# Three-stage kernel: attention's small matmuls with PE's halves in turn, and leaky relu kept in the PSUM bank of h

## The chip, the cores and the metric

The kernel runs on one core of a Trainium2 chip. Its time is the device time of one execution in microseconds (us); the kernel before was run three times for the median, and one further execution was profiled.

## The reference

Input are q, k, v of 4 batches x 8 heads x 576 positions x 64, and the weights of two MLP layers ("MoE 1" and "MoE 2") of width 512 -> 2048 -> 512, in float64. What is computed, cut to what matters:

```python
scores = (q @ k.T) / 8                          # per batch and head
rel = pos[:, None] - pos[None, :]
plain   = (rel >= 0) & (rel < 32)               # heads 0 to 3
dilated = (rel >= 0) & (rel < 128) & (rel % 4 == 0)   # heads 4 to 7
x = softmax(where(mask, scores, -1e9)) @ v      # -> 2304 tokens x 512

h = x @ w_in1                                   # MoE 1: 2304 x 2048
g = maximum(h, 0) + alpha * minimum(h, 0)       # leaky relu, one slope per column
x = g @ w_out1

h = x @ w_in2                                   # MoE 2
g = (a0 + a1 h + a2 h^2 + a3 h^3) / (1 + |b0||h| + |b1|h^2 + 1e-6)
out = g @ w_out2
```

## The kernel before

The matmuls of the MLP layers run in a fast fp32 format, each operand split in a high and a low part, so that every product is three matmuls (low x high, high x low, high x high). Attention's matmuls run in plain fp32; each of them appears in the trace as two.

**Chunks and jobs.** The 2304 tokens are cut in 8 chunks of 288 (u = 0 to 7). One attention job (`attention_job`, a generator with a `yield` between its stages) does one pair of heads of one chunk: `hp` 0 and 1 are plain, 2 and 3 dilated. Its stages are: load q and k; turn them with PE (L354 to L364); copy them to SBUF on ScalarE (ACT); load v; scores; row maxima on VectorE (DVE, `maxima`, L421); exponentials on ACT; row sums inverted on DVE and applied on GpSimd (POOL, `norm`); turn the weights with PE (`turn`); copy (`turned`); P V (L500 to L514); split the result in the high and low part of x1 (L523, L524).

**Scores.** A dilated job has 4 blocks per head; each head has its own PSUM bank, and `scores(0)` and `scores(1)` are separate stages. A head lies on 64 of the 128 partitions, so its matmuls use half of PE's rows (64 x 72 weights, with 72 columns for even u and 104 for odd u). A plain job has 5 blocks; both heads are done by one matmul each, with the queries of the two heads in `qz`, a 128 x 128 block with zeros off its diagonal halves: `scores(0)` does all, `scores(1)` nothing.

**P V.** Both heads write to one bank, head 0 to partitions 0 to 63 and head 1 to 64 to 127, that is with the two halves of PE's columns. All matmuls of head 0 are issued ahead of those of head 1.

**MoE 1.** A step n is one block f of 128 hidden columns of one chunk (`SEQ`). `half1(n, 0)` issues the 12 matmuls of h (`moe1_h`), `half1(n, 1)` the 12 of y for step n - 2 (`moe1_y`). The leaky relu of a step is four instructions: `turned` (ACT, sign * h to SBUF tile r), `larger` (DVE, the maximum of h * slope and r), `hi` (ACT, rounded high part), `lo` (DVE, the low part). h lies in one of two PSUM banks with the tag "h"; the bank is free again when its last reader is done.

**Order.** Attention's stages are hung between the half steps: `STEPS` gives their offset in half steps from the start of a job, `BASES` the start of each job in its chunk; stages of PE (`ON_PE`) stand behind the half step's MoE matmuls, the others ahead of them. The jobs of u = 0 run in the head, in the order of `HEAD`, and those of u = 1 and 2 are hung closer (`EARLY`). In steady running the scores of a job fall in the same half step as the P V of the job before; banks with the tag "att" (two) serve both. The weights of MoE 1 are decoded from float64 on DVE (L151 to L164) in the first part, those of MoE 2 at a slower pace behind. Within this order a planner of the framework places each engine's instructions by its own cost estimates and by free buffers, and adds the waits. MoE 2 (L950 on) is written out by hand.

Of the kernel before, what the change touches and what calls it, by code (L numbers as in the profile page):

```python
# [8 lines left out]
F32 = mybir.dt.float32  # L9
F32R = mybir.dt.float32r  # L10
I32 = mybir.dt.int32
AF = mybir.ActivationFunctionType
ALU = mybir.AluOpType
# [9 lines left out]
def tile_attention_moe_moe2(  # L23
# [14 lines left out]
    nc = tc.nc  # L38
    B, H, S, D = q.shape
# [5 lines left out]
    P = 128  # L45
    KD = DM // P
    NF = DFF // P
    C1 = 288
# [25 lines left out]
    QS = 56  # L74
# [23 lines left out]
    def bank(tag, bufs, name):  # L98
        return psum.tile([P, 512], F32, tag=tag, bufs=bufs, name=name)
# [133 lines left out]
    def mem_att(nm):  # L233

        two = (("tq", "tk") if AHEAD == 2 else ()) + ("tv", "mx", "sm", "rs")

        def f(tag, shape):
            if tag == "qz":
                return qz0
            return att.tile(  # L240
                shape, F32, tag=tag, name=f"{tag}{nm}", bufs=2 if tag in two else 1
            )

        return f

    def mem_head(nm, dil, qz):

        if dil:
            at = {"tq": (0, 0), "tk": (0, 512), "tv": (1, 0), "qT": (1, 512),
                  "kT": (2, 0), "pT": (2, 416), "pr": (3, 0)}  # L250
        else:
            at = {"tq": (0, 0), "qz": (0, 384), "tv": (1, 0), "kT": (1, 640),
                  "tk": (2, 0), "pr": (2, 512), "pT": (3, 0)}
        ts = [
            wpool.tile([P, 2 * DM], F32, tag=("wh", "wl")[i % 2], name=f"hd{nm}_{i}")
            for i in range(4)
        ]

        def f(tag, shape):
            if tag not in at:  # L260
                return att.tile(shape, F32, tag=tag + "h", name=f"{tag}{nm}", bufs=KD)
            if tag == "qz" and qz is not None:
                return qz
            i, c0 = at[tag]
            n = 1
            for d in shape[1:]:
                n *= d
            t = ts[i][: shape[0], c0 : c0 + n]
            if len(shape) == 3:
                t = t.rearrange("p (a b) -> p a b", a=shape[1])  # L270
            elif len(shape) == 4:
                t = t.rearrange("p (a b c) -> p a b c", a=shape[1], b=shape[2])
            if tag == "qz":
                zero_qz(t)
            return t

        return f

    def zero_qz(t):
        nc.vector.memset(t[:D, :, 1, :], 0.0)  # L280
        nc.vector.memset(t[D:, :, 0, :], 0.0)


    def attention_job(mem, u, hp, bk, eng=nc.sync, split=False):

        b, t0 = divmod(u * C1, S)
        dil = 2 * hp >= H // 2
        h0 = 2 * hp
        nm = f"{u}_{hp}"
        first = t0 == 0  # L290
        if dil:
            nb, bq = 4, C1 // 4
            kw = bq if first else bq + W
            groups = ((0, 1, 2, 3), (4, 5, 6, 7))
            rows, span = bq, kw
            tq = mem("tq", [bq, 2, 4 * D])
# [17 lines left out]
        else:  # L314


            nb, bq = 3, 96
            groups = ((0, 1, 2), (3, 4))
            rows, span = P, 96
            back = 0 if first else W  # L320
            key = [max(0, QS * j - W + back) for j in range(5)]
            k_rows = 96 if first else 80
            nk = (C1 + back) // k_rows
            tq = mem("tq", [bq, nb, 2, D])
# [29 lines left out]
        pq = bk(f"pq{nm}")  # L354
# [9 lines left out]
            )  # L364
        yield
        kT = mem("kT", [P, kn * k_rows])
        if dil:
            qT = mem("qT", [P, C1])
            nc.scalar.activation(qT, pq[:, :C1], AF.Copy)
        else:  # L370


            qz = mem("qz", [P, 5, 2, 64])
            for h in range(2):
                src = pq[h * D : (h + 1) * D, :64]
                src = bass.AP(src.tensor, src.offset, [src.ap[0], [QS, 5], [1, 64]])
                nc.scalar.activation(qz[h * D : (h + 1) * D, :, h, :], src, AF.Copy)
        nc.scalar.activation(kT, pk[:, : kn * k_rows], AF.Copy)
        yield
        if dil:  # L380
            tv = mem("tv", [kw, 2, 4 * D])
            load(tv, v, True)
        else:
            tv = mem("tv", [span, 5, 2, D])
# [11 lines left out]
        sm = mem("sm", [rows, nblk])  # L396
        ps = [None, None]

        def scores(g):
            if dil:  # L400

                ps[g] = bk(f"ps{nm}_{g}")
                r = slice(g * D, (g + 1) * D)
                for c in range(nb):
                    nc.tensor.matmul(  # L405
                        ps[g][:bq, c * kw : (c + 1) * kw],
                        lhsT=qT[r, c * bq : (c + 1) * bq],
                        rhs=kT[r, c * kw : (c + 1) * kw],
                        start=True, stop=True,
                    )  # L410
            elif g == 0:
                ps[0] = ps[1] = bk(f"ps{nm}")
                for j in range(5):
                    nc.tensor.matmul(  # L414
                        ps[0][:, j * span : (j + 1) * span],
                        lhsT=qz[:, j].rearrange("p h i -> p (h i)"),
                        rhs=kT[:, key[j] : key[j] + span],
                        start=True, stop=True,
                    )

        def maxima(g):  # L421
            for j in groups[g]:
# [41 lines left out]
        def turned(g):  # L464
# [2 lines left out]
                AF.Copy,  # L467
            )

        scores(0)  # L470
        yield
        maxima(0)
        yield
        scores(1)
        yield
        exponentials(0)
        yield
# [20 lines left out]
            turned(g)  # L498
        yield
        px = bk(f"px{nm}")  # L500
        for h in range(2):
            for j in range(4 if dil else 5):
                if dil:
                    lhsT = tv[:, h, j * D : (j + 1) * D]
                    at, n = (j % 2 * 4 + 2 * h + j // 2) * bq, bq
                    to = j * bq
                else:
                    lhsT = tv[:, j, h, :]
                    n, to = QS if j < 4 else 64, j * QS
                    at = j * P + h * 64  # L510
                nc.tensor.matmul(  # L511
                    px[h * D : (h + 1) * D, to : to + n],
                    lhsT=lhsT, rhs=pT[:, at : at + n], start=True, stop=True,
                )  # L514
# [13 lines left out]
    def h_matmuls(ph, n, w_h, w_l, xh, xl):  # L528
        i = 0
        for c in range(KD):  # L530
            for w_, x_ in ((w_l, xh), (w_h, xl), (w_h, xh)):
                nc.tensor.matmul(  # L532
                    ph[:, :n], lhsT=w_[:, c * P : (c + 1) * P], rhs=x_[:, c, :],
                    start=(i == 0), stop=(i == 3 * KD - 1),
                )
                i += 1

    if True:
# [4 lines left out]
        def pair(name, n):  # L543

            return (
                gy.tile([P, C2], F32R, tag="hi", name=f"{name}h")[:, :n],
                gy.tile([P, C2], F32R, tag="lo", name=f"{name}l")[:, :n],
            )

        a1 = ExitStack()  # L550
        att = a1.enter_context(tc.tile_pool(name="att", bufs=1, side="right"))
# [14 lines left out]
        def x1_tiles(u):  # L566
# [4 lines left out]

        x1 = {}

        qz0 = att.tile([P, 5, 2, 64], F32, name="qz0")
        zero_qz(qz0)

        hb = bk_any()
        first_jobs = [
            attention_job(
                mem_head(f"0_{hp}", 2 * hp >= H // 2, qz0 if hp == 0 else None),  # L580
                0, hp, hb, nc.gpsimd if hp in POOLJ else nc.sync, SPLIT,
            )
            for hp in HPS
# [2 lines left out]
        for _ in range(WARM):  # L586
            nc.tensor.matmul(warm[:, :P], lhsT=ident, rhs=ident, start=True, stop=True)
        jobs = [
            attention_job(mem_att(f"{u}_{hp}"), u, hp, bk_att)
            for u in range(1, NC1) for hp in range(KD)  # L590
        ]
# [48 lines left out]
        def at_half(n, half, fn):  # L640
            later.setdefault((n, half), []).append(fn)

        def moe1_h(n):
            u, f = SEQ[n]
            ph = bank("h", 2, f"h1_{u}_{f}")
            h_matmuls(ph, C1, wh[1, f], wl[1, f], *x1[u])
            h = ph[:, :C1]
            r = mo1.tile([P, C1], F32, tag="r1", name=f"r1_{u}_{f}", bufs=3)
            ghi, glo = pair(f"g1_{u}_{f}", C1)
            g_tiles[n] = (ghi, glo)  # L650
            sg, sa = side[:, f : f + 1], salpha[:, f : f + 1]

            def turned():
                nc.scalar.activation(r, h, AF.Identity, scale=sg)  # L654

            def larger():
                nc.vector.scalar_tensor_tensor(r, h, sa, r, op0=ALU.mult, op1=ALU.max)  # L657

            def hi():
                nc.scalar.activation(ghi, r, AF.Identity, scale=sg)  # L660

            def lo():
                nc.vector.scalar_tensor_tensor(
                    glo, r, sg, ghi.bitcast(F32), op0=ALU.mult, op1=ALU.subtract
                )

            at_half(n, 1, turned)
            at_half(n, 1, larger)
            at_half(n + 1, 0, hi)
            at_half(n + 1, 1, lo)  # L670
# [324 lines left out]
```

## Time and profile before

| | |
|---|---|
| median of 3 runs | 998.19 us (996.92 to 1001.0) |
| profiled execution | 995.79 us, of which span 993.9 us |
| mean granted TensorE clock | 0.979 |
| PE busy | 955.2 us (96%) |
| DVE busy | 690.7 us (69%) |
| ACT busy | 644.4 us (65%) |
| POOL busy | 283.7 us (29%) |
| chain that ended last | PE 80%, DVE 10%, DMA 3%, ACT 3% |

The span is the time from the first to the last instruction. Busy time is the time in which an engine had at least one instruction under way; PE's matmuls overlap, so each of them lasts longer than the distance between two. The chain is followed back from the last instruction, at each step to what released it.

### The profile page before, as it was taken

The page shows a single profiled execution, that of the slowest core. Times are in us where ns is not written, and L with a number is a line of the kernel's source. Part 1 is how long each engine was busy: PE and PEld are TensorE (multiplying, and loading weights), DVE is VectorE, ACT ScalarE, POOL GpSimd, SP SyncE. Part 2 cuts the span into 40 slices and gives each one's busy share as a digit, 9 for nine tenths or more (in the row PEclk, how much of TensorE's full clock was granted, in tenths as well). Part 3 has the DMA queues.
Part 4 walks back from the last instruction along what each step waited for, and adds up shares of the span by engine and source line. Part 5 has one row for each costly group of instructions (what it writes and reads, how often), then busy time and mean ns, then how long its engine had stood idle before and what let it go on. Part 6 is the DMA issues. An engine that isn't in the chain of part 4 may idle for free.

```text
span 993.9 us, 18304 instructions
## 1 busy us (share of the span) xinstructions
PE 955.2 (96%) x6544; PEld 894.2 (90%) x6544; DVE 690.7 (69%) x1633; ACT 644.4 (65%) x1608; POOL 283.7 (29%) x329
## 2 busy tenths in 40 slices
PE   6678889999999999999999999999999999999998
PEld 6567879999999999999999999999999999999996
DVE  5999975565555555654444669877777777777776
ACT  3677555666565665664554578776777776776775
POOL 3455430100001010100011335434343343343332
PEclk7599999999999999999999999999999999999999
DMA  8465642564453642621206433002002030020000
GB/s 206 122 189 155 191 135 88 167 196 141 118 174 93 181 140 85 198 71 35 92 4 197 148 130 89 1 33 64 1 33 64 1 96 1 33 64 1 33 1 32
DMA packets 93930, 94.38 MB, mean 95 GB/s; under 512 B 40208, under 2 KB 81680, under 8 KB 93840
## 3 DMA queue, kind: packets, MB, share of 16 engines
q1 hardware_dynamic: 87392, 83.78, 28.0%
q0 software_dynamic: 6448, 9.45, 3.8%
q8 instruction: 51, 0.84, 0.4%
q14 instruction: 39, 0.32, 0.1%
HBM read 69.48 MB, written 23.72 MB: 94 GB/s over the span
## 4 chain that ended last, share of the span: by engine, by line
PE 80%; DVE 10%; DMA 3%; ACT 3%; issue 3%; POOL 0%; SPq 0%; POOLq 0%; ACTq 0%; DVEq 0%
PE h L532 36%; PE o L908 19%; PE y L687 16%; PE px L511 3%; DMA raw<-in_moe_w_in_dram 2%; DVE w L158 2%; DVE w L164 2%; PE ps L405 2%; PE pp L459 1%; DVE w L151 1%; PE ps L414 1%; DMA raw<-in_moe_w_out_dram 1%; DVE r L657 1%; DVE wl L228 1%; PE pk L362 1%
## 5 line engine op out<-in xcount | busy, mean ns | idle before, releaser
L532 PE MATMUL h<-x1h,wl 128*128 128x288 f32 x512 | 157.4, 308 | 4.4 <-DVE r L657 4.4
L532 PE MATMUL h<-x1l,wh 128*128 128x288 f32 x512 | 152.3, 298 | 0.0
L532 PE MATMUL h<-x1h,wh 128*128 128x288 f32 x512 | 151.8, 296 | 0.0
L657 DVE SCALAR_TENSOR_TENSOR r<-h,salpha,r 128x288 f32<-128x288 f32 x128 | 65.8, 514 | 110.8 <-ACT r L654 110.5
L448 POOL TENSOR_TENSOR pr<-pr,sm 72x416 f32<-72x416 f32 (+3 forms) x56 | 41.1, 753 | 350.8 <-DVE sm L444 281.8
L532 PE MATMUL h<-x2h,wl 128*128 128x384 f32 x384 | 130.4, 340 | 0.0
L532 PE MATMUL h<-x2h,wh 128*128 128x384 f32 x384 | 130.0, 339 | 0.0
L532 PE MATMUL h<-x2l,wh 128*128 128x384 f32 x384 | 129.6, 338 | 0.0
L840 POOL TENSOR_SCALAR qq<-hh,babs 128x384 f32<-128x384 f32 x96 | 56.7, 591 | 225.7 <-ACT hh L838 225.6
L654 ACT ACTIVATE r<-h,side 128x288 f32<-128x288 f32 x128 | 63.5, 496 | 80.2 <-PE h L532 79.9
L532 PEld LDWEIGHTS h<-x1h,wl 128*128 128x128 f32 x512 | 96.7, 189 | 7.9 <-DVE r L657 2.4
L843 POOL TENSOR_TENSOR qq<-qq,w 128x384 f32<-128x384 f32 x96 | 97.8, 1019 | 8.0
L532 PEld LDWEIGHTS h<-x1l,wh 128*128 128x128 f32 x512 | 97.0, 189 | 0.3 <-DVE x1l L524 0.2
L532 PEld LDWEIGHTS h<-x1h,wh 128*128 128x128 f32 x512 | 97.0, 189 | 0.2
L838 ACT ACTIVATE hh<-h 128x384 f32<-128x384 f32 x96 | 47.2, 492 | 63.0 <-PE h L532 62.4
L845 DVE TENSOR_TENSOR t<-h,t 128x384 f32<-128x384 f32 x96 | 53.5, 557 | 48.6 <-ACT t L844 48.3
L532 PEld LDWEIGHTS h<-x2h,wl 128*128 128x128 f32 x384 | 72.0, 188 | 4.0
L532 PEld LDWEIGHTS h<-x2l,wh 128*128 128x128 f32 x384 | 72.1, 188 | 3.6
L854 ACT ACTIVATE w<-qq 128x384 f32<-128x384 f32 (+1 forms) x98 | 51.0, 520 | 33.2 <-POOL qq L843 33.2
L532 PEld LDWEIGHTS h<-x2h,wh 128*128 128x128 f32 x384 | 72.0, 187 | 0.0
L436 ACT ACTIVATE pr<-pr,mx 128x96 f32<-128x96 f32 (+2 forms) x182 | 65.2, 359 | 9.6 <-DVE mx L428 9.5
L862 DVE TENSOR_TENSOR qq<-qq,w 128x384 f32<-128x384 f32 (+1 forms) x98 | 54.2, 553 | 24.4 <-ACT w L857 24.1
(365 smaller groups left out, 2704.5 us busy)
## 6 DMA issues: line engine op xcount, KB each, us to landing
raw<-in_moe_w_in_dram SPq DMA_DIRECT2D x32, 512.0 KB
raw<-in_moe_w_out_dram SPq DMA_DIRECT2D x32, 512.0 KB
w2f<-w SPq DMA_DIRECT2D x32, 256.0 KB
w<-w2f SPq DMA_DIRECT2D x16, 512.0 KB
x2h<-x2hi POOLq DMA_DIRECT2D x6, 768.0 KB, 5.0
x2l<-x2lo POOLq DMA_DIRECT2D x6, 768.0 KB, 6.2
out_dram<-o SPq DMA_DIRECT2D x15, 256.0 KB
tq<-in_q_dram SPq DMA_DIRECT2D x28, 72.0 KB
```

Source lines behind the costliest of these rows:

```text
L436: nc.scalar.activation(pr[:, j, :], pr[:, j, :], AF.Exp, scale=-1.0, bias=mx[:, j : j + 1], accum_out=sm[:, j : j + 1],)
L532: nc.tensor.matmul(ph[:, :n], lhsT=w_[:, c * P : (c + 1) * P], rhs=x_[:, c, :], start=(i == 0), stop=(i == 3 * KD - 1),)
L654: nc.scalar.activation(r, h, AF.Identity, scale=sg)
L657: nc.vector.scalar_tensor_tensor(r, h, sa, r, op0=ALU.mult, op1=ALU.max)
L687: nc.tensor.matmul(ys[c][:, :C1], lhsT=w_[:, s], rhs=g_, start=begin and i == 0, stop=end and i == 2,)
L838: nc.scalar.activation(hh, h, AF.Square)
L840: nc.gpsimd.tensor_scalar(qq, hh, babs, 1.0 + 1e-6, op0=ALU.mult, op1=ALU.add)
L843: nc.gpsimd.tensor_tensor(qq, qq, w, op=ALU.add)
L845: nc.vector.tensor_tensor(t, h, t, op=ALU.mult)
L854: nc.scalar.activation(w[:, s], qq[:, s], AF.Abs_reciprocal_sqrt, scale=2.0**-44)
L862: nc.vector.tensor_tensor(qq[:, s], qq[:, s], w[:, s], op=ALU.mult)
L908: nc.tensor.matmul(o2[c][i], lhsT=g_, rhs=w_, start=(f == 0 and j == 0), stop=(f == NF - 1 and j == 2),)
```

## The change

Four edits. The dilated scores of both heads are issued in one stage, block by block with the heads in turn, each head to its own bank; the second stage stays as an empty `yield`. The plain scores become two 64 x 64 matmuls per block, head 0 and head 1 in turn, and `qz` with its zeros goes: q is copied to `qT` by one instruction as in the dilated case. P V is issued block by block with the heads in turn. In MoE 1 `larger` writes its result back to the PSUM bank of h, and `hi` and `lo` read it there.

```diff
-        if dil:
-            qT = mem("qT", [P, C1])
-            nc.scalar.activation(qT, pq[:, :C1], AF.Copy)
-        else:
-            qz = mem("qz", [P, 5, 2, 64])
-            for h in range(2):
-                src = pq[h * D : (h + 1) * D, :64]
-                src = bass.AP(src.tensor, src.offset, [src.ap[0], [QS, 5], [1, 64]])
-                nc.scalar.activation(qz[h * D : (h + 1) * D, :, h, :], src, AF.Copy)
+        qT = mem("qT", [P, C1])
+        nc.scalar.activation(qT, pq[:, :C1], AF.Copy)
...
-        def scores(g):
+        def scores():
             if dil:
-                ps[g] = bk(f"ps{nm}_{g}")
-                r = slice(g * D, (g + 1) * D)
+                ps[:] = [bk(f"ps{nm}_{g}") for g in range(2)]
                 for c in range(nb):
-                    nc.tensor.matmul(
-                        ps[g][:bq, c * kw : (c + 1) * kw],
...
+                    for g in range(2):
+                        r = slice(g * D, (g + 1) * D)
+                        nc.tensor.matmul(
+                            ps[g][:bq, c * kw : (c + 1) * kw],
+                            lhsT=qT[r, c * bq : (c + 1) * bq],
+                            rhs=kT[r, c * kw : (c + 1) * kw],
+                            start=True, stop=True,
+                        )
-            elif g == 0:
-                ps[0] = ps[1] = bk(f"ps{nm}")
+            else:
+                ps[:] = [bk(f"ps{nm}")] * 2
                 for j in range(5):
-                    nc.tensor.matmul(
-                        ps[0][:, j * span : (j + 1) * span],
-                        lhsT=qz[:, j].rearrange("p h i -> p (h i)"),
...
+                    for h in range(2):
+                        r = slice(h * D, (h + 1) * D)
+                        nc.tensor.matmul(
+                            ps[0][r, j * span : (j + 1) * span],
+                            lhsT=qT[r, j * QS : j * QS + 64],
+                            rhs=kT[r, key[j] : key[j] + span],
+                            start=True, stop=True,
+                        )
...
-        scores(0)
+        scores()
         yield
         maxima(0)
         yield
-        scores(1)
         yield
...
-        for h in range(2):
-            for j in range(4 if dil else 5):
+        for j in range(4 if dil else 5):
+            for h in range(2):
...
             def larger():
-                nc.vector.scalar_tensor_tensor(r, h, sa, r, op0=ALU.mult, op1=ALU.max)
+                nc.vector.scalar_tensor_tensor(h, h, sa, r, op0=ALU.mult, op1=ALU.max)
             def hi():
-                nc.scalar.activation(ghi, r, AF.Identity, scale=sg)
+                nc.scalar.activation(ghi, h, AF.Identity, scale=sg)
             def lo():
                 nc.vector.scalar_tensor_tensor(
-                    glo, r, sg, ghi.bitcast(F32), op0=ALU.mult, op1=ALU.subtract
+                    glo, h, sg, ghi.bitcast(F32), op0=ALU.mult, op1=ALU.subtract
                 )
```

## Rows read from the trace of the kernel before

**Rows 1.** Busy us by stage: PE, PEld, DVE, ACT, POOL; then clock, DMA.
```profile
97.00:146.00 49.00, 41.56 (x296) 39.07 (x296) 44.73 (x62) 29.27 (x59) 21.27 (x14) 1.00 0.57 170
146.00:230.00 84.00, 82.33 (x712) 79.31 (x711) 47.59 (x169) 51.98 (x162) 7.53 (x12) 1.00 0.51 150
...
432.00:498.00 66.00, 66.00 (x567) 64.30 (x566) 31.21 (x110) 36.11 (x113) 5.59 (x8) 1.00 0.23 65
```

**Rows 2.** The chain of waits, 28 to 60 us: start, us, what.
```profile
37.38 3.85 PE px L511 x40
```

**Rows 3.** Timeline of PE, 307 us: start us, us, engine, line, what, count.
```profile
307.29 0.29 PE L532 MATMUL h<-x1h,wh 128*128 128x288 f32 x1
307.52 0.73 PE L405 MATMUL ps<-kT,qT 64*72 64x72 f32 x8
308.18 0.40 PE L687 MATMUL y<-g_7h,wl 128*128 128x288 f32 x1
```

**Rows 4.** The same, 310 us.
```profile
309.73 0.29 PE L687 MATMUL y<-g_7h,wh 128*128 128x288 f32 x1
309.96 1.02 PE L511 MATMUL px<-pT,tv 72*64 72x72 f32 x16
310.91 0.73 PE L405 MATMUL ps<-kT,qT 64*72 64x72 f32 x8
311.57 0.40 PE L532 MATMUL h<-x1h,wl 128*128 128x288 f32 x1
```

**Rows 5.** Timeline of PE around 16 and around 20 matmuls of P V.
```profile
321.63 0.29 PE L687 MATMUL y<-g_10h,wh 128*128 128x288 f32 x1
...
322.80 0.40 PE L532 MATMUL h<-x1h,wl 128*128 128x288 f32 x1
...
348.90 0.29 PE L687 MATMUL y<-g_1h,wh 128*128 128x288 f32 x1
...
350.25 0.40 PE L532 MATMUL h<-x1h,wl 128*128 128x288 f32 x1
```

**Rows 6.** Timeline of PE, 359 us (104 columns).
```profile
359.35 0.29 PE L532 MATMUL h<-x1h,wh 128*128 128x288 f32 x1
359.57 0.93 PE L405 MATMUL ps<-kT,qT 64*72 64x104 f32 x8
360.43 0.40 PE L687 MATMUL y<-g_4h,wl 128*128 128x288 f32 x1
```

**Rows 7.** Timeline of PE, 188 us (u = 2).
```profile
187.59 0.29 PE L687 MATMUL y<-g_11h,wh 128*128 128x288 f32 x1
187.81 1.06 PE L405 MATMUL ps<-kT,qT 64*72 64x72 f32 x16
188.79 0.40 PE L687 MATMUL y<-g_11h,wl 128*128 128x288 f32 x1
```

**Rows 8.** Timeline of PE around 10 matmuls of plain scores.
```profile
334.46 0.29 PE L532 MATMUL h<-x1h,wh 128*128 128x288 f32 x1
...
335.62 0.38 PE L687 MATMUL y<-g_14h,wl 128*128 128x288 f32 x1
```

**Rows 9.** Timeline of DVE, 309 us.
```profile
309.34 0.52 DVE L663 SCALAR_TENSOR_TENSOR g_9l<-r,side,g_9h 128x288 fp32r<-128x288 f32 x1
```

**Rows 10.** Groups of DVE: shapes, count | busy us, mean ns | idle before.
```profile
L657 DVE SCALAR_TENSOR_TENSOR r<-h,salpha,r 128x288 f32<-128x288 f32 x128 | 65.8, 514 | 110.8 <-ACT r L654 110.5
L846 DVE SCALAR_TENSOR_TENSOR h<-t,ab,h 128x384 f32<-128x384 f32 x96 | 59.8, 623 | 3.5
```

**Rows 11.** Timelines of PE and DVE, 138 to 140 us; idle before, releaser.
```profile
138.52 0.37 PE L532 MATMUL h<-x1h,wl 128*128 128x288 f32 x1 [1.12 <-DVE r L657]
...
139.07 1.24 DVE L663 SCALAR_TENSOR_TENSOR g_8l<-r,side,g_8h 128x288 fp32r<-128x288 f32 x1 [0.70 <-ACT g_8h L660]
```

**Rows 12.** Timelines of PE and DVE, 578 us.
```profile
578.30 0.29 PE L532 MATMUL h<-x1h,wl 128*128 128x288 f32 x1
...
578.51 0.52 DVE L663 SCALAR_TENSOR_TENSOR g_13l<-r,side,g_13h 128x288 fp32r<-128x288 f32 x1 [0.60 <-ACT g_13h L660]
```

More of the change, by code (lines that the diff above doesn't have):

```diff
@@ L237, in f @@
         def f(tag, shape):
-            if tag == "qz":
-                return qz0
             return att.tile(
@@ L244, in mem_att, with mem_head @@
         return f
-    def mem_head(nm, dil, qz):
+    def mem_head(nm, dil):
         if dil:
@@ L251, in mem_head @@
         else:
-            at = {"tq": (0, 0), "qz": (0, 384), "tv": (1, 0), "kT": (1, 640),
+            at = {"tq": (0, 0), "qT": (0, 384), "tv": (1, 0), "kT": (1, 640),
                   "tk": (2, 0), "pr": (2, 512), "pT": (3, 0)}
@@ L261, in f @@
                 return att.tile(shape, F32, tag=tag + "h", name=f"{tag}{nm}", bufs=KD)
-            if tag == "qz" and qz is not None:
-                return qz
             i, c0 = at[tag]
@@ L272, in f @@
                 t = t.rearrange("p (a b c) -> p a b c", a=shape[1], b=shape[2])
-            if tag == "qz":
-                zero_qz(t)
-            return t
-        return f
-    def zero_qz(t):
-        nc.vector.memset(t[:D, :, 1, :], 0.0)
-        nc.vector.memset(t[D:, :, 0, :], 0.0)
+            return t
+        return f
     def attention_job(mem, u, hp, bk, eng=nc.sync, split=False):
@@ L397, in attention_job @@
         ps = [None, None]
-        def scores(g):
+        def scores():
             if dil:
-                ps[g] = bk(f"ps{nm}_{g}")
-                r = slice(g * D, (g + 1) * D)
+                ps[:] = [bk(f"ps{nm}_{g}") for g in range(2)]
                 for c in range(nb):
-                    nc.tensor.matmul(
-                        ps[g][:bq, c * kw : (c + 1) * kw],
[L407 to L410, printed above, removed]
-            elif g == 0:
-                ps[0] = ps[1] = bk(f"ps{nm}")
-                for j in range(5):
-                    nc.tensor.matmul(
-                        ps[0][:, j * span : (j + 1) * span],
-                        lhsT=qz[:, j].rearrange("p h i -> p (h i)"),
-                        rhs=kT[:, key[j] : key[j] + span],
-                        start=True, stop=True,
-                    )
+                    for g in range(2):
[8 more added lines that the diff above has]
+                ps[:] = [bk(f"ps{nm}")] * 2
+                for j in range(5):
+                    for h in range(2):
[6 more added lines that the diff above has]
+                        )
         def maxima(g):
@@ L572, in tile_attention_moe_moe2 @@
         x1 = {}
-        qz0 = att.tile([P, 5, 2, 64], F32, name="qz0")
-        zero_qz(qz0)
         hb = bk_any()
@@ L579, in tile_attention_moe_moe2 @@
             attention_job(
-                mem_head(f"0_{hp}", 2 * hp >= H // 2, qz0 if hp == 0 else None),
+                mem_head(f"0_{hp}", 2 * hp >= H // 2),
                 0, hp, hb, nc.gpsimd if hp in POOLJ else nc.sync, SPLIT,
```

## The prediction

> **What bounds the kernel now.** I read the page's engine shares first, then its 40 slices, and then the busy time of each engine by stage, since an average over stages hides which engine ends last in each. The reader is to see three stages. From about 146 us to the end TensorE (PE) is the bound: 82.33 of 84 us busy in the first stretch and 66.00 of 66 in a later one [rows 1]. From about 48 to 146 us VectorE (DVE) is: in the second half of it DVE is busy 44.73 of 49 us and PE only 41.56 [rows 1]; the weights of the first layer are decoded there. Before 48 us the four first attention jobs run, and the chain of waits shows PE on it for a while, 3.85 us for the 40 matmuls of two jobs' P V [rows 2]. MoE 2, from about 590 us, is written out by hand and the change touches none of it.
>
> So attention's small matmuls cost time only where PE is the bound, and there in full. I took their price from the timeline of PE: **the cost of a burst** is the start of the first MoE matmul behind it, less the start of the last one ahead of it, less 0.13 us, the distance of two MoE matmuls. After 146 us lie the jobs of u = 2 to 7: 12 plain ones and 12 dilated ones.
>
> **The change, part by part.**
>
> *Dilated scores.* Each of the two heads of a job has 8 matmuls (4 blocks, each run as two). Today the heads are two bursts with an MoE half step between. At 72 columns the first costs 308.18 - 307.29 - 0.13 = 0.76 us [rows 3]. The second stands behind 16 matmuls of P V: together 311.57 - 309.73 - 0.13 = 1.71 [rows 4], and 16 of P V alone cost 322.80 - 321.63 - 0.13 = 1.04 [rows 5], so 0.67 is the second's. At 104 columns the first costs 360.43 - 359.35 - 0.13 = 0.95 [rows 6], the second by the same difference 0.86.
>
> The rows show what the two halves of PE can do side by side. Where the two bursts happen to be adjacent, 16 matmuls cost 188.79 - 187.59 - 0.13 = 1.07 us [rows 7], not 1.43: the second head starts while the first still runs, and adds 0.31. If the heads alternate from the first matmul on, I expect both to run in the time of one: 0.76 and 0.95. Saved: (1.43 - 0.76) = 0.67 for 4 jobs, (1.81 - 0.95) = 0.86 for 6 jobs, and 1.07 - 0.76 = 0.31 for the 2 jobs of u = 2, whose bursts are adjacent already: 2.7 + 5.2 + 0.6 = 8.5 us. Bounds: if the alternation gives no more than today's adjacent bursts do, (1.43 - 1.07) = 0.36 for 10 jobs, 3.6 us; no overlap at all is the fourth rival.
>
> *P V.* 16 matmuls (dilated) cost 1.04 us, 20 (plain) 350.25 - 348.90 - 0.13 = 1.22 [rows 5]. They are already two heads in the two halves of PE's columns, one after the other. Half of the 16 is a burst of 8 at 72 columns, 0.76 as above; half of the 20 is ten at 56 columns, which at 0.045 for each more matmul (1.22 - 1.04 over 4) makes about 0.85. Saved 0.28 x 12 + 0.37 x 12 = 7.8 us. Bounds: 0, and 1.04 / 2 and 1.22 / 2, which would be 13.6.
>
> *Plain scores.* Five 128 x 128 blocks, half of them zeros, become ten 64 x 64 ones: 20 matmuls instead of 10. Today 10 cost 335.62 - 334.46 - 0.13 = 1.03 us [rows 8]. If the quarters of PE overlap as the halves do, this is a burst of ten at 96 columns: between 0.76 and 0.95 for eight, so 0.90, and two more at some 0.08 ((0.95 - 0.76) / 8 = 0.024 for 32 columns, three times that for 96), 1.07. Cost 0.04 x 12 = 0.5 us. No row shows such quarters, so the other bound is twenty in a row, 1.07 + 10 x 0.08 = 1.9 us, 10 us in all. I take the first, because the two heads read and write separate partitions, as the halves of [rows 7] do. The two copies into qz become one into qT on ScalarE, which PE doesn't wait for; worth nothing here.
>
> *The moved half of the dilated scores.* It now takes both attention banks at once, and P V of the job before must wait until the first head's maxima have left theirs. DVE has done them when it starts the next low part, at 309.34 [rows 9]; P V starts at 309.96 [rows 4]. The MoE half step between (12 matmuls, 1.56 us) covers the wait by 0.6 us. Price 0; without that cover at most some 0.5 us for each of 12, 6 us.
>
> *Leaky relu in PSUM.* `larger` now writes to PSUM. Today it takes 514 ns; an instruction of that form with 384 columns that does write to PSUM takes 623 [rows 10], which for 288 columns means between 623 x 288 / 384 = 467 (all of it goes by width) and 623 (none of it). I take 520, near what `larger` takes itself: nothing; the other end, 0.11 us, would count only in the 17 steps of the decode stage, 2 us. `lo` loses one of its two SBUF inputs; one of them took 1.24 us [rows 11], where `larger`, with the same width and one SBUF input, stays at 0.51.
>
> The Trainium skill (Perfetto Trace Analysis, Optimizing Scalar/DVE Operations) speaks against this edit: DVE's access overhead is higher on PSUM (about 125 ns) than on SBUF (about 60). By it two instructions of each step would lose 65 ns, an estimate of 2.2 us for the 17 steps where DVE is the bound. By the widths of [rows 10] it would be near nothing, so the sum leaves it out.
>
> What the edit does cost is the **bank of h**. There are two; h of step n + 2 needs the bank of step n, which is now held until `lo` of step n has read it, instead of until `larger` has. In the stage that PE bounds this is covered: `lo` in [rows 9] ends at 309.86, while the next block of h starts at 311.57 [rows 4] and isn't even the one that needs this bank. Two places are not covered. In the decode stage h starts before that `lo` is over: at 138.52, against 139.07 + 1.24 = 140.31 [rows 11], 1.8 us early. There PE waits for DVE anyway (7.4 us idle of 49), so a later h costs only what is left of the lag when the stage ends, up to 1.8 us. At the end of MoE 1, h starts at 578.30 and `lo` ends at 579.03 [rows 12]: 0.7 us, and less if `hi`, reading PSUM, shortens the loop.
>
> *Early part.* The first jobs' P V, 3.85 us for 40, could lose 0.3 of it, 1.1 us, and shorter `lo` some 2 to 4 us of DVE; against it stand the 1.8 us. I take -1.0, between +3 and -5.
>
> **Sum:** -8.5 - 7.8 + 0.5 - 1.0 + 0.3 = -16.5 us. The profiled execution took 995.79 us (span 993.9 and 1.9 around it), so 979.3. The median of the three runs, 998.19, lies 2.4 above that execution, which gives 981.7 for it; I say 981.
>
> **The rivals.**
>
> 1. *Alternating is slower than full overlap.* Mechanism: PE's instruction stream, and not its array, sets the pace of the alternating bursts. If they went no faster than today's adjacent ones [rows 7], P V would save nothing and the dilated scores 3.6 us; halfway between that and full overlap the gain is (8.5 + 7.8 - 3.6) / 2 = 6.4 us smaller, -10, and the time 988. For it: no row shows more than a few alternating matmuls in a row. Against: in [rows 7] the second head adds less than half of what a burst costs. Chance 12%, 985 to 993. The Trainium skill (TensorE: Matmul & The Clock Gate, Measured speedup vs the span model) gives 3.07 times for four row tiles, three quarters of the ideal; by that share an estimate of the gain is 12 us, 986.
>
> 2. *The quarters don't overlap*, though the halves do: 10 us on the plain scores, -16.5 + 10 = -6.5, 991. Chance 8%.
>
> 3. *The bank of h decides (slower).* Place: the 17 first steps of MoE 1, 48 to 146 us. Each h waits for the `lo` two steps ahead, and each later h makes a later `larger`, behind which the decode of the weights stands in DVE's queue; if DVE idles for it, the delay isn't absorbed. Price: at the 1.8 us of [rows 11] for each of 17 steps 31 us, 998 + 31 - 16.5 = 1013 in full; it decides from the point where more than half isn't absorbed. For it: PE did wait for `larger` there, 1.12 us ahead of 138.52 [rows 11]. Against: DVE does a whole step's decode between `lo` of n and `larger` of n + 2. Half absorbed, 6%: 998. In full, 7%: 1013.
>
> 4. *No overlap at all:* the halves take turns without running together. Plain scores +10, P V and dilated scores as today, -16.5 + 10 + 7.8 + 8.5 = +10: 1008. The 0.31 us of the second head speaks against it [rows 7]. Chance 4%.
>
> **How the numbers follow.** Main case 63%: 973 to 987, its width from the early part (+3 to -5 about its -1) and the P V bounds. Rival 1 12%, rival 2 8%, rival 3 13%, rival 4 4%. The range 973 to 995 holds the main case, rivals 1 and 2: about 82%. A measurement of this kernel tells 0.5% from no change, 993.2 and 1003.2. Faster: 63 + 11 + 6 = 80%; same: 10%; slower: 10%.
>
> **What would show it.** Right: in the timeline a dilated job has one burst of 16 scores that costs 0.76 or 0.95 us, and none behind P V; P V costs near 0.76 and 0.85; plain scores of 20 matmuls cost near 1.07; PE still busy without gaps from 146 us on; MoE 2 starts about 16 us earlier and takes as long as before. Wrong: bursts that cost as much as today; plain scores of 1.5 us or more; PE waiting for `lo` ahead of h before 146 us with DVE's busy share falling there; or P V waiting for maxima.

## The result, and the profile after

The kernel after takes 975.57 us (median of 4, 975.20 to 977.26); the kernel before took 998.24 beside it (median of 4, 996.92 to 1001.0). The ratio is 0.9773, interval 0.9749 to 0.9796: 22.7 us faster, where the forecast was 981 and -16.5. Measured again beside other kernels it was 976.76 against 996.43, ratio 0.9805 (0.9788 to 0.9822), 19.7 us. The sign and the mechanism were forecast; the size was not quite, and the parts were off more than the sum.

The page of after, engine shares and part of the 40 slices:

```profile
PE 932.1 (96%) x6704; PEld 869.2 (89%) x6704; DVE 680.2 (70%) x1629; ACT 630.2 (65%) x1592; POOL 282.0 (29%) x329
...
PE   5678889998999999999999999999999999999998
...
PEclk8599999998999999999999999999999999999999
```

PE is busy for 23 us less, and the bound is where it was. New is the tenth slice (from 220 us), in which PE and the clock both dip.

The spans of the two profiled executions differ by 18.4 us. By landmarks (start of the first matmul of h of a step, in us):

| from the start of | before | after | the stretch got |
|---|---|---|---|
| span to h of step 0 | 44.96 | 42.17 | -2.79 |
| to h of step 20 (end of the stage that DVE bounds) | 146.16 | 139.10 | -4.27 |
| to h of step 42 | 246.18 | 240.10 | +0.98 |
| to h of step 112 (last attention job is done) | 530.60 | 513.03 | -11.49 |
| to MoE 2 | 581.48 | 564.37 | +0.46 |
| to the end | 993.87 | 975.46 | -1.30 |

The profiled execution of before (995.79) lies under all four timed ones, that of after (977.26) is the longest of its four; that is the difference between 18.4 and 22.7. One more thing stands out: the early part gave 7.06 us, forecast 1.0, and the stretch from step 20 to 42, in which jobs have shorter bursts too, gave nothing in this execution; the stall below is why.

**The bursts.** Timeline of PE of after; columns as in [rows 3]. At 299 us a dilated job's scores (72 columns) and the next P V, which answer to [rows 3, 4]:

```profile
299.53 0.29 PE L518 MATMUL h<-x1h,wh 128*128 128x288 f32 x1
299.75 0.74 PE L389 MATMUL ps<-kT,qT 64*72 64x72 f32 x16
300.42 0.40 PE L671 MATMUL y<-g_7h,wl 128*128 128x288 f32 x1
...
301.98 0.29 PE L671 MATMUL y<-g_7h,wh 128*128 128x288 f32 x1
302.20 0.72 PE L497 MATMUL px<-pT,tv 72*64 72x72 f32 x16
302.85 0.40 PE L518 MATMUL h<-x1h,wl 128*128 128x288 f32 x1
```

Sixteen scores cost 300.42 - 299.53 - 0.13 = 0.76 us, what 8 cost before; P V costs 302.85 - 301.98 - 0.13 = 0.74. No scores stand behind P V. Next 104 columns, which answer to [rows 6], and plain scores, which answer to [rows 8]:

```profile
350.06 0.29 PE L518 MATMUL h<-x1h,wh 128*128 128x288 f32 x1
350.29 0.94 PE L389 MATMUL ps<-kT,qT 64*72 64x104 f32 x16
351.16 0.40 PE L671 MATMUL y<-g_4h,wl 128*128 128x288 f32 x1
```

```profile
325.46 0.29 PE L518 MATMUL h<-x1h,wh 128*128 128x288 f32 x1
325.68 1.04 PE L401 MATMUL ps<-kT,qT 64*64 64x96 f32 x20
326.65 0.40 PE L671 MATMUL y<-g_14h,wl 128*128 128x288 f32 x1
```

They cost 0.97 and 1.06 us. P V of 20, at 340 us, costs 0.83.

**The stall at 221 us.** PE, DVE and ACT of after, and the windows around it (columns as in [rows 1]):

```profile
220.88 0.30 PE L671 MATMUL y<-g_4h,wh 128*128 128x288 f32 x1
224.17 1.33 PE L497 MATMUL px<-pT,tv 96*64 96x56 f32 x20 [2.99 <-DVE mx L415]
225.43 0.61 PE L518 MATMUL h<-x1h,wl 128*128 128x288 f32 x1
```

```profile
222.86 0.53 DVE L641 SCALAR_TENSOR_TENSOR h<-h,salpha,r 128x288 f32<-128x288 f32 x1 [6.22 <-ACT r L638]
```

```profile
221.79 0.65 ACT L146 ACTIVATE raw<-raw 128x512 f32<-128x512 f32 x1 [4.20 <-DMA raw<-in_moe_w_out_dram]
222.35 0.48 ACT L638 ACTIVATE r<-h,side 128x288 f32<-128x288 f32 x1
```

```profile
219.00:224.00 5.00, 2.18 (x22) 1.82 (x18) 1.14 (x8) 1.61 (x4) 0.00 (x0) 0.92 0.24 66
224.00:229.00 5.00, 4.83 (x35) 4.71 (x36) 3.19 (x15) 3.21 (x16) 0.00 (x0) 0.50 0.39 112
```

Read upwards: ACT's queue stands for 4.20 us behind weights of MoE 2 that have not landed; behind them waits `turned`, behind that on DVE `larger`, and behind that in DVE's queue the maxima of the scores issued at 218 us. P V needs the bank that these maxima free, and PE idles for 2.99 us. The granted clock then is 0.50, the 1.2 GHz level, from 224 to 229 us. This is the bank wait that the forecast priced at 0; it cost 3.6 us in the burst and, at half clock, about 2 more (the next 19 matmuls stand some 0.24 us apart instead of 0.13).

**The early part.** DVE was busy for 125.2 us up to h of step 20 before and is busy for 118.4 now: 6.8 us less against 7.06 us of time. Where the largest piece comes from is seen on `lo`. The view of one line of DVE, durations min/median/max in ns, first of before (L663), then of after (L647):

```profile
L663 DVE SCALAR_TENSOR_TENSOR g_1l<-r,side,g_1h x2: 510/1028/1545, 60.5 to 108.8; 128x288 fp32r<-128x288 f32 x2
...
L663 DVE SCALAR_TENSOR_TENSOR g_5l<-r,side,g_5h x2: 512/1032/1552, 91.4 to 125.3; 128x288 fp32r<-128x288 f32 x2
```

```profile
L647 DVE SCALAR_TENSOR_TENSOR g_1l<-h,side,g_1h x2: 505/512/518, 57.3 to 102.8; 128x288 fp32r<-128x288 f32 x2
...
L647 DVE SCALAR_TENSOR_TENSOR g_5l<-h,side,g_5h x2: 502/504/506, 82.5 to 118.7; 128x288 fp32r<-128x288 f32 x2
```

In before five `lo` of the first 20 took 0.93 to 1.55 us, together 3.9 us over the 0.51 of the others; in after none takes more than 0.52. All 20 took 14.0 us before and 10.2 after (the 10.8 and 7.7 of the expectation below are the first 15). PE does wait for `lo` ahead of h now, nine times; the two largest of the groups (waits of PE from 42 to 139 us: sum, times, longest):

```profile
PE h L518 <- DVE g_7l L647: 2.1, 2, 1.2
...
PE h L518 <- DVE g_4l L647: 1.3, 1, 1.3
```

These waits take 6.4 us in all, in a stage that DVE bounds: the `lo` of steps 7 to 16 each end only 0.1 to 0.2 us before the h that needs their bank begins. A second execution of this kernel ("the kernel after once more", below) reaches step 20 at 140.93, so it has 5.23 us of early gain and not 7.06; the granted clock from step 0 to 20 is 0.93 in it and 0.96 here.

### The profile page after: what moved, and what is told of

Same layout as the page of the kernel before. It is cut to its first block, busy times and chain, and to the rows that moved or that the text cites. A ratio compares the mean times of both kernels' runs of the same rounds, so it can differ in the third digit from the quotient of the medians.

```text
span 975.5 us, 18667 instructions
## 1 busy us (share of the span) xinstructions
PE 932.1 (96%) x6704; PEld 869.2 (89%) x6704; DVE 680.2 (70%) x1629; ACT 630.2 (65%) x1592; POOL 282.0 (29%) x329
## 4 chain that ended last, share of the span: by engine, by line
PE 82%; DVE 8%; ACT 4%; DMA 3%; issue 2%; POOL 1%; SPq 1%; POOLq 0%; DVEq 0%; ACTq 0%
PE h L518 38%; PE o L892 20%; PE y L671 18%; DMA raw<-in_moe_w_out_dram 2%; DVE w L158 2%; PE px L497 2%; DVE w L164 1%; PE pp L446 1%; DMA raw<-in_moe_w_in_dram 1%; DVE w L151 1%; PE ps L401 1%; ACT pr L423 1%; PE ps L389 1%; ACT raw L146 1%; POOL pr L435 1%
## 5 line engine op out<-in xcount | busy, mean ns | idle before, releaser
L641 DVE SCALAR_TENSOR_TENSOR h<-h,salpha,r 128x288 f32<-128x288 f32 x128 | 66.7, 521 | 115.5 <-ACT r L638 115.5
```

The costliest lines, as they stand in the source:

```text
L641: nc.vector.scalar_tensor_tensor(h, h, sa, r, op0=ALU.mult, op1=ALU.max)
```

## The experiments

Each was timed in five rounds (`hold` in three) against the kernel before on the same chip, which took 996.3 to 997.3 us there. Theory A: the halves of PE overlap as forecast, and the early part gained more because `lo` lost its second SBUF input. Theory B: the early gain came from attention, through the first jobs.

**The leaky relu alone.**

```diff
-                nc.vector.scalar_tensor_tensor(r, h, sa, r, op0=ALU.mult, op1=ALU.max)
+                nc.vector.scalar_tensor_tensor(h, h, sa, r, op0=ALU.mult, op1=ALU.max)
...
-                nc.scalar.activation(ghi, r, AF.Identity, scale=sg)
+                nc.scalar.activation(ghi, h, AF.Identity, scale=sg)
...
-                    glo, r, sg, ghi.bitcast(F32), op0=ALU.mult, op1=ALU.subtract
+                    glo, h, sg, ghi.bitcast(F32), op0=ALU.mult, op1=ALU.subtract
```

> The kernel before with the leaky relu edit alone. Theory A (the early part, before 146 us, gained more than forecast because the low part of the leaky relu lost its second SBUF input): in the trace of after the first 20 lo took 7.7 us in place of 10.8 and DVE was the engine that set the pace there, so 4 to 5 us go, 993.5 us, all of it ahead of the point where the 20th block of h starts. Theory B (the early gain came from attention's edits, through the first jobs): 997 to 999 us, and h of the 20th block starts at 146 us as before. Both: no change in the stage behind it, nor in MoE 2.

992.07 us against 997.3, ratio 0.9950 (0.9938 to 0.9963): -5.2, near the 4 to 5 of theory A. Where the 5.2 lie its trace doesn't show. The profiled execution (993.07, the longest of its five) is only 2.6 us shorter in span than before's; h of step 20 starts at 144.41, 1.75 us earlier, and MoE 2 gives 1.3. So "all of it ahead of the 20th block" was a miss in the trace. The stretch from step 0 to 20, of before, of this kernel, of attention's edits alone (a run further down) and of after (columns as in [rows 1]):

```profile
44.96:146.16 101.20, 84.82 (x643) 77.33 (x643) 94.05 (x184) 68.21 (x172) 46.10 (x34) 0.97 0.56 168
```

```profile
44.16:144.41 100.25, 88.63 (x644) 83.16 (x643) 88.41 (x184) 67.96 (x172) 45.98 (x34) 0.89 0.56 169
```

```profile
42.71:142.01 99.30, 80.92 (x665) 73.98 (x663) 92.58 (x185) 66.83 (x170) 45.42 (x34) 0.97 0.58 172
```

```profile
42.17:139.10 96.93, 81.40 (x665) 74.60 (x663) 88.82 (x185) 66.58 (x170) 46.48 (x34) 0.96 0.59 176
```

With the leaky relu alone DVE is busy for 5.6 us less, but it idles for 11.8 us where it idled for 7.2, and PE's granted clock is 0.89 where it was 0.97: most of the busy time saved became idle time there. Whether PE's waits for `lo` or the clock did that, one trace can't tell.

What is shown is why `lo` got shorter. This trace has the same meeting of `lo` with a subtraction of POOL as before's. DVE and POOL of before:

```profile
60.48 1.54 DVE L663 SCALAR_TENSOR_TENSOR g_1l<-r,side,g_1h 128x288 fp32r<-128x288 f32 x1
```

```profile
60.35 2.83 POOL L187 TENSOR_TENSOR wl<-w,wh 128x512 fp32r<-128x512 f32 x2 [2.98 <-ACT wh L181]
```

and of this kernel:

```profile
60.42 0.51 DVE L663 SCALAR_TENSOR_TENSOR g_1l<-h,side,g_1h 128x288 fp32r<-128x288 f32 x1
60.85 1.36 DVE L164 SCALAR_TENSOR_TENSOR w<-raw,w 128x512 int32<-128x512 int32 x1
```

```profile
60.28 3.08 POOL L187 TENSOR_TENSOR wl<-w,wh 128x512 fp32r<-128x512 f32 x2 [3.19 <-ACT wh L181]
```

With both inputs in SBUF `lo` takes 1.54 us beside POOL's subtraction; with one in PSUM it takes 0.51 beside the same subtraction. The decode instruction behind it, both inputs in SBUF, still pays (1.36 us here, 1.78 in before, and 0.68 when it meets none). The same holds for all of the first 20 steps: in before the five `lo` that start while a POOL instruction runs are the five long ones, and in after the five that do take 0.52 at most. "No change in MoE 2" was a miss: in the six kernels without this edit MoE 2 takes 412.3 to 412.4 us in the profile, in all with it 411.1 to 411.3. Without it PE waits, in MoE 2's first block, for the low part of MoE 1's last result; why the edit ends this wait was not tried. PE of before, then of after:

```profile
594.11 0.50 PE L908 MATMUL o<-wl,g_0h 128*128 128x512 f32 x1 [0.84 <-DVE y_0l L720]
```

```profile
576.01 0.39 PE L892 MATMUL o<-wl,g_0h 128*128 128x512 f32 x1
```

**The same for steps 20 to 127 alone.**

```diff
+            m = h if n >= 20 else r
...
-                nc.vector.scalar_tensor_tensor(r, h, sa, r, op0=ALU.mult, op1=ALU.max)
+                nc.vector.scalar_tensor_tensor(m, h, sa, r, op0=ALU.mult, op1=ALU.max)
```

(`hi` and `lo` read m.)

> The kernel before with the leaky relu edit for steps 20 to 127 alone, those behind the stage that DVE bounds. Theory A (lo's second SBUF input cost DVE 4 us in the first 20 steps and nothing behind): no change, 996.5 to 998. Rival (the edit pays in every step, through ScalarE or a shorter loop): 992 to 994, as the whole edit.

995.36 against 996.43, ratio 0.9993 (0.9982 to 1.0005): no change that can be told. Ten `lo` behind step 20 took 0.66 to 1.09 us in before, for the same reason; here none takes more than 0.52, and where PE is the bound that is worth nothing. By difference most of the 5.2 belongs to the first 20 steps, as theory A says; the profile of the whole edit has 1.75 there.

**Attention's edits alone** (the kernel after with `larger`, `hi` and `lo` as before).

```diff
-                nc.vector.scalar_tensor_tensor(h, h, sa, r, op0=ALU.mult, op1=ALU.max)
+                nc.vector.scalar_tensor_tensor(r, h, sa, r, op0=ALU.mult, op1=ALU.max)
```

> The changed kernel with the leaky relu edit undone, so attention's three edits alone. Theory A: the kernel after without the 4 to 5 us of the early part, 980 us, between 979 and 982. Theory B: within 1 us of the kernel after, 975 to 977. Both: the bursts cost what they cost in the kernel after (0.96 us for 16 scores of 104 columns, 0.82 for 20 of P V).

980.15 (977.16 to 983.41) against 997.3, ratio 0.9828 (0.9805 to 0.9850): -17.2. The time is theory A's figure, and the two halves of the change add up: 5.2 + 17.2 = 22.4. The profile speaks for theory B as well: h of step 20 starts at 142.01, 4.15 us earlier than in before. In single executions attention's edits thus have 4.15 of the early gain and the leaky relu 1.75, together 5.9 beside the 7.06 and 5.23 of after; neither theory is right alone. This execution, too, has a stall of P V behind maxima at 225 us, shorter and without a fall of the clock:

```profile
227.07 0.80 PE L497 MATMUL px<-pT,tv 96*64 96x56 f32 x20 [1.83 <-DVE mx L415]
```

**P V's order alone.**

```diff
-        for h in range(2):
-            for j in range(4 if dil else 5):
+        for j in range(4 if dil else 5):
+            for h in range(2):
```

> The kernel before with P V's order alone changed, block by block with the heads in turn. If the halves of PE's columns overlap: 0.28 us x 12 + 0.37 x 12 = 7.8 us in the stage that PE bounds, about 1 more in the first jobs if theory B holds, so 989.5 to 990.5. If the order of issue doesn't matter (overlap as in the kernel before): 998.

987.77 against 997.3, ratio 0.9904 (0.9889 to 0.9919): -9.5, somewhat more than the 7.8 and 1. In its profile the bursts cost 0.74 and 0.82, and h of step 0 starts 2.15 us earlier: more than the 1.1 that the forecast had for the first jobs' P V; at h of step 20 1.16 us of it is left.

**The dilated scores alone**, one stage and heads in turn, and then one stage with head after head:

```diff
+                if g == 1:
+                    return
-                ps[g] = bk(f"ps{nm}_{g}")
-                r = slice(g * D, (g + 1) * D)
+                ps[:] = [bk(f"ps{nm}_{e}") for e in range(2)]
                 for c in range(nb):
+                    for e in range(2):
```

```diff
-                for c in range(nb):
-                    for e in range(2):
+                for e in range(2):
+                    for c in range(nb):
```

> The kernel before with the dilated scores alone changed: one stage, heads in turn. Full overlap: 8.5 us, 989.7. If one stage without the turn is all that counts: 3.6 us, 994.6. If P V of the job before then waits for maxima in each of 12 jobs at 0.5 us: 6 us less of a gain, and PE idle ahead of P V in the trace.

> The kernel before with the dilated scores of both heads in one stage, but all 8 matmuls of head 0 ahead of those of head 1. If the turn is what lets the halves run together: a burst of 16 costs 1.07 us at 72 columns and about 1.3 at 104, so 0.36 to 0.5 x 10 = 3.6 to 5 us less than before, 993; the version in turn had 988.6. If one stage is enough: 988 to 989.5, and a burst of 16 costs 0.76 and 0.95.

In turn 988.61 against 997.3, ratio 0.9910 (0.9896 to 0.9924): -8.7, full overlap. Head after head 992.23 against 996.43, ratio 0.9955 (0.9943 to 0.9968): -4.2. PE of the latter:

```profile
307.18 0.29 PE L535 MATMUL h<-x1h,wh 128*128 128x288 f32 x1
307.40 1.06 PE L408 MATMUL ps<-kT,qT 64*72 64x72 f32 x16
308.39 0.40 PE L690 MATMUL y<-g_7h,wl 128*128 128x288 f32 x1
```

The same 16 matmuls cost 1.08 us here and 0.76 in turn. About half of the gain is that one burst replaces two, the other half the turn.

**Plain scores as before, the rest as after** (`qz`, its copies and its memsets stay):

```diff
-                    for h in range(2):
-                        r = slice(h * D, (h + 1) * D)
-                        nc.tensor.matmul(
-                            ps[0][r, j * span : (j + 1) * span],
+                    nc.tensor.matmul(
+                        ps[0][:, j * span : (j + 1) * span],
+                        lhsT=qz[:, j].rearrange("p h i -> p (h i)"),
```

> The changed kernel without its third edit: plain scores as before, 10 matmuls of 128 x 128 with zeros in qz, and the two memsets of qz again; the other edits as in the kernel after. If the quarters overlap fully (burst of 20 at 1.06 us against 1.03): 0.4 us faster behind 146 us, less 0.6 to 1.2 us that the memsets and two copies in place of one cost in the first part, so within 1 us of the kernel after, 974.5 to 976. Rival (the quarters bring more than forecast, since attention alone gave 17.2 us and P V and dilated scores alone 9.5 and 8.7): 2 us or more slower than the kernel after. Other side (quarters cost more than the burst shows): 973 or less, and then this is the faster version.

972.70 (972.53 to 973.09) against 996.43, ratio 0.9759 (0.9747 to 0.9772); the kernel after beside it 976.76 (975.61 to 980.07). It beats both kernels, the one after by 4 us, and the two intervals (0.9788 to 0.9822 for after) don't meet: the quarters are a loss, and more than the 0.03 us of a burst explain (1.06 against 1.03; counted to the fifth MoE matmul behind, 1.16 against 1.11, 0.6 us over 12 jobs). In the profiles after is 4.6 us longer than this version, and its stall at 221 us alone is 5.6; its second execution, next, is 3.0 longer, 1.4 of that ahead of step 20 and 1.0 in waits for q.

**The kernel after once more.** The edit is none.

> The changed kernel once more, beside the others of this chip. 975 to 976. Its trace answers whether P V's wait of 3.0 us for maxima at 224 us (behind a late transfer of weights, followed by 5 us at half clock) belongs to the kernel or to that one execution: if to the kernel, PE idles again ahead of the P V of u = 2 that stands near 224 us; if not, the 39th block of h starts near 223 and not 225.4.

Here PE has no wait for maxima behind 139 us; its longest is another, for q at 215 us. Waits of PE from 139 to 600 us:

```profile
PE pq L348 <- DMA tq<-in_q_dram: 1.6, 1, 1.6
PE pp L446 <- POOL pr L435: 0.7, 2, 0.5
```

So the stall of 2.99 us belongs to that execution: what the kernel has is a place where a late transfer reaches PE. The second half of the forecast missed: h of step 39 starts at 225.02, since this execution had lost 3 us before that step in other ways.

**Where the quarters cost: u = 3 to 7 alone, and u = 0 to 2 alone.**

```diff
+        quarter = not dil and u >= 3
-        if dil:
+        if dil or quarter:
             qT = mem("qT", [P, C1])
```

```diff
-        quarter = not dil and u >= 3
+        quarter = not dil and u < 3
```

> The version with wide plain scores (972.7 us), but quarters of 64 x 64 in the plain jobs of u = 3 to 7, those that run where PE is the bound. Bursts of 20 cost 1.06 in place of 1.03 us there (1.16 and 1.11 when the fifth MoE matmul behind is counted too): 0.3 to 0.5 us for 10 jobs, 973 to 973.5. That is theory C, by which the 4 us between this version and the kernel after come from the jobs of u = 0 to 2. Rival D, the burst costs more than its ends show (4 us over 12 jobs, 0.33 each): 975.5 to 976.5.

> The complement: quarters in the plain jobs of u = 0 to 2 alone, the wide form behind. Theory C: 975.5 to 976.5, as the kernel after. Rival D: 973 to 974. If neither edit alone brings the 4 us, they come from the order that the planner finds for the whole, and no share can be given to a place.

975.82 (974.02 to 976.34) and 974.83 (972.97 to 978.52), against 996.26. Ratios 0.9789 (0.9775 to 0.9802) and 0.9789 (0.9767 to 0.9810). The first is at theory D's figure, the second between C's and D's, so neither theory has both: no place has the 4 us to itself. In the profile of the first, most of what it lost to the wide version is one stall, again behind a late weight transfer in ACT's queue. PE, then ACT:

```profile
283.64 0.29 PE L547 MATMUL h<-x1h,wh 128*128 128x288 f32 x1
285.67 1.01 PE L409 MATMUL ps<-kT,qT 64*72 64x72 f32 x16 [1.74 <-ACT pT L480]
```

```profile
284.20 0.65 ACT L146 ACTIVATE raw<-raw 128x512 f32<-128x512 f32 x1 [3.20 <-DMA raw<-in_moe_w_in_dram]
```

**P V and dilated scores in turn, without the quarters and the leaky relu** (the two edits above together).

> The kernel before with P V and the dilated scores in turn, without the quarters and without the leaky relu edit. It gives the price of the quarters a second time, free of the other edit: attention's three edits together took 980.15 us, 17.2 less than before. If the quarters cost the 0.4 us of their bursts: 979.5 to 980.5. If they cost the 3 to 4 us that the version with wide scores gained: 976 to 977. By the sum of the single edits (9.5 + 8.7 off 996.5): 978.3.

977.84 (975.03 to 979.23) against 996.79, ratio 0.9804 (0.9781 to 0.9828): -19.0, where attention's three edits gave -17.2. The intervals overlap; by this pair the quarters cost about 2 us, by the other 4.

**`lo` hung one half step later** (the kernel after):

```diff
-            at_half(n + 1, 1, lo)
+            at_half(n + 2, 0, lo)
```

> The kernel after with the low part hung one half step later, which keeps the bank of h longer: from one half step behind hi to the half step in which the next h of that bank starts. It doubles the suspected wait of the third rival. If the wait is absorbed (DVE runs lo as soon as hi is done, wherever it is hung, and PE has 12 matmuls of y to go): 976 to 979, with PE without gaps behind 146 us. If the bank of h decides: 0.5 us or more of PE's idle time ahead of each h behind 146 us, 108 steps, 1030 us or more.

979.04 (977.39 to 981.25) against 996.26, ratio 0.9828 (0.9811 to 0.9844): 2 to 3.5 us slower than after. Where PE is the bound it has no gap:

```profile
424.00:490.00 66.00, 66.00 (x617) 63.66 (x614) 29.37 (x107) 34.86 (x111) 5.27 (x8) 1.00 0.21 61
```

In its profile the way from step 0 to 20 takes 100.1 us, where after took 96.9 and 98.9; the granted clock there is 0.91, against 0.96 and 0.93. But the edit didn't make `lo` later: between steps 40 and 112 `lo` ends 3.4 us (median) ahead of the h that needs its bank, and 3.5 us in after. So no longer hold was tested. What both traces show is that in steady running the bank is free with 3 us to spare.

## Why the prediction was right

*Dilated scores, forecast 0.76 and 0.95, -8.5.* Right: 0.76 and 0.97 in the trace, -8.7 alone. The bound 3.6 is what head after head gives (-4.2), so the choice between the bounds was the turn.

*P V, forecast 0.76 and 0.85, -7.8.* Right: 0.74 and 0.83; with the first jobs, which the forecast counted in the early part, -9.5. Rival 1 (the alternation goes slower than full overlap) falls, and with it its estimate by the Trainium skill (TensorE: Matmul & The Clock Gate, Measured speedup vs the span model): two halves in turn gave the whole factor of two here, not three quarters. Rival 4 falls with it.

*Plain scores, forecast 1.07, +0.5.* The burst is right (1.06), so rival 2 falls; the edit's price is not: it costs 2 to 4 us. The burst explains 0.4 to 0.6. What the rest is stays open: in the traces it is stalls behind late transfers and time ahead of step 20, both of which differ from execution to execution, and no run shows that the quarters cause them.

*The moved half, price 0, up to 6.* Right in steady running, where the wide version and after's second execution show no wait above 0.2 us, and wrong at 221 us: the half step that covers the wait covers 0.6 us, not a transfer that is 4.2 us late. The bound held: 5.6 us in one execution, 1.8 in the attention version, 0.2 in the wide version, none in after's second.

*Leaky relu in PSUM, price 0 for `larger`.* Right: 521 ns instead of 514 [rows 10]. `hi`, reading PSUM, takes 0.50 us instead of 0.54. The Trainium skill's higher overhead of DVE on PSUM (Perfetto Trace Analysis, Optimizing Scalar/DVE Operations) is not seen here: 7 ns, not 65, and `lo` costs 0.52 either way where nothing meets it.

*Bank of h, up to 1.8 and 0.3.* Rival 3's price falls (31 us slower in full), its mechanism only in part: PE does wait for `lo` before step 20, 6.4 us, and DVE idles between steps 0 and 20 for 8.1 us in after, 7.2 in before and 11.8 with the leaky relu alone. At the end of MoE 1 the stretch from step 112 got 0.46 longer, near the 0.3; MoE 2 gave 1.3 back.

*Early part, -1.0: the term that was mis-sized.* It measured 7.06 and 5.23 us in after's two profiles. It set 1.1 us of P V and 2 to 4 us of shorter `lo` against 1.8 us of bank wait and kept 1. In the profiles of the parts the leaky relu alone has 1.75, which is what its terms allow (3.9 us of shorter `lo`, and a wait that took part of it back); attention's edits alone have 4.15, where 1.1 was put, and of P V's order alone only 1.16 is left at step 20. So by the profiles it is attention's share that was too small. By the timings it is the leaky relu's, with 5.2 us in all, 1.3 of them in MoE 2, where the forecast had nothing. The two don't agree, and why attention's edits shorten the early part beyond P V stays open. With the edits as they were timed singly the sum is -5.2 - 9.5 - 8.7 + 2 to 4 = -21.4 to -19.4, near the two measurements (-22.7 and -19.7).

That the time lay only some 5 us from the forecast is in part luck: in the profile the early part gave 6 us more than forecast and MoE 2 1.3 more, and the stall at 221 us, priced at 0, took 5.6 back.

Summed by kind from the timelines, attention's bursts behind step 20 gave 8.2 us for scores, 8.2 for P V and -0.3 for plain scores in after (stall left out): 16.1, forecast 15.8.

## What to carry to other kernels

Small matmuls that use half of PE's rows or columns should be issued with the halves in turn: 16 of them cost 1.08 us here with one half after the other, and 0.76 in turn, as much as 8. Price each edit in the engine that bounds the stage: shorter `lo` were worth nothing where PE was the bound. Where DVE was, look at what became of the time saved: with the leaky relu alone 5.6 us of DVE's busy time went, and in the profiled execution it idled 4.7 us more. And time each part of a bundle by itself, and look in its trace whether the gain lies where you think: here the one that split a full 128 x 128 matmul into quarters took back 2 to 4 us of what the others gave.

## What the runs showed that was not expected

A DVE instruction with two inputs in SBUF takes 1.54 us instead of 0.51 when it starts while POOL works on SBUF operands of its own; with one of its inputs in PSUM it takes 0.51 beside the same POOL instruction. And 20 matmuls on 64 x 64 quarters of PE, both heads writing to one bank, cost 1.06 us, where 10 on the whole array with the same columns cost 1.03: the quarters cost what the forecast had for full overlap (1.07) and still save nothing against blocks half of which are zeros.
